# An attention with two expert layers: a weight quarter of the second layer converted earlier, GpSimd's pairs planned as longer, and the whole order planned anew

## The chip, the core and the metric

The kernel runs on one core of a Trainium2 chip. Its engines work side by side, each through its own queue in order: TensorE (PE, matmuls, with PEld its weight loads), VectorE (DVE), ScalarE (ACT), GpSimd (POOL) and SyncE (SP, whose queue here issues transfers). The metric is the device time of one execution in microseconds; before the change it is 805.47 us (median of 3 runs, 804.94 to 806.22).

## The reference

The input is a batch of 2 with 8 heads, 768 rows and 64 columns a head: 16 heads in all, counted 0 to 15 below. A row may attend to a column only if both fall into the same of 64 buckets, which six signs of a projection name. Two expert layers follow on the 1536 tokens of width 512, each with an inner width of 2048:

```python
    scores = np.where(mask, scores, -1000000000.0)
    attn = np.exp(scores - max); attn = attn / (sum + 1e-09)
    x = attn @ v                                  # 1536 x 512
    h = x @ w_in;  g = np.maximum(h, 0) + alpha * np.minimum(h, 0);  x = g @ w_out
    h = x @ w_in2; g = P(h) / (Q(h) + 1e-06);                        out = g @ w_out2
```

P is a cubic and Q a sum of absolute terms up to the square. The weights are float32.

## The kernel before

**Attention.** For each head: `load` of q and k (L428), copies rounded for TensorE (`qh`, `k2`) and their remainders (`ql`, `kx`), a small matmul for the bucket bits (`pb`, L440), whose signs VectorE writes as `bt` (L445) and two pairs of small transfers put beside `ql` and `k2` (L456). For each of six row blocks of 128: scores (`s`, L508 and L510), VectorE's scaling and minimum into `x` (`clamp`, L516), ScalarE's exponential (L522), the turn by TensorE (`t`, L540), and the copy out of PSUM into `pt` (`put`, L398 on ScalarE, L402 on VectorE). Then the product with v (`pv`, L600, 24 matmul records a head) and, on VectorE, its product with the reciprocal sums `rs` into the accumulator `acc` (`over`, L606). Heads 0 to 7 are the first batch, 8 to 15 the second.

**Expert layers.** The tokens stand in four blocks of 384 (`c` = 0 to 3), the inner width in four quarters (`Q`). One block with one quarter is a unit: four groups of twelve matmuls `h` (L626), each followed by the layer's function, its rounded result `gh` and remainder `gl` (L407), then the second product (L642 in layer one: four groups of twelve; L645 in layer two: three groups of twelve) and its sum into `acc` (L752). Every product is made of three, high x high, high x low and low x high, so each weight is split into a high and a low part. The block of tokens is split in the same way (`xh`, `xl`). Blocks 0 and 1 are complete after the first batch, so the first two units of layer one (8 groups of first and 8 of second products) can run inside the second batch; block 2 and 3 need the last head.

**Layer two's function** (`act2`) needs twelve steps for each 128 x 384 tile; two of them, the pair `a_mul` and `a_sum` (L691), have both inputs in SBUF and may run on VectorE or GpSimd.

**Conversion.** A piece is 128 x 512 weights. It is loaded (`raw`, L297), ScalarE takes two steps (L303, L307), VectorE five `bits` steps (L316, L318, L320, L322, L324) and the low part (L331); the high part is a copy. Pieces of layer one's quarters go straight into the two weight slots. Pieces of layer two's quarters 1 to 3 (kind `f`) are written out to DRAM (`spill`, two transfers, L341) and loaded back as a whole when their slot is free (`reload`, L851). They are listed in groups of eight pieces before the first unit of layer one's quarters 1, 2 and 3, and run beside its units and on into layer two.

**Order.** Nothing is ordered by hand: `Plan.order` (L159) lists every step with its engines, the time it is planned to take there, its buffers and its dependences, and lays the steps out one after the other by a rank plus a bias for each kind of step (table `FAVOUR`, from L62, with factors on the planned time by engine). Steps marked `dve` and `pool` may not overlap in the plan (`PORT`); steps marked `dvp` may. The order so found is written into each engine's queue.

Of the kernel before, what the change touches and what calls it, by code (L numbers as in the profile page):

```python
# [31 lines left out]

SCALE = 0.125
# [34 lines left out]
    "bits0": (90.6, {"pe": 3.82}), "bits_at": (-21, {"dvp": 3}), "bits_ev": (-33.5, {"dvp": 0.62}),
    "bits_evb": (-78.9, {"dvp": 0.26}), "bits_mv": (-44, {"dma": 1.35}), "bits_mvb": (-4.7, {"dma": 0.6}),
    "bitsb": (-0.2, {}), "c_abs": (-7.3, {"act": 4.44}), "c_bits": (-9.8, {"dve": 1.83}),  # L70
    "c_hi": (-117.1, {"act": 1.07, "dve": 0.06, "pool": 0.99}), "c_lo": (46.3, {}),
    "c_load": (-3, {"none": 1.84, "dma": 0.23}), "c_prep": (-65.8, {"dve": 0.95}), "c_tail": (11.2, {"act": 2.79}),
    "clamp": (23.3, {"dvp": 1.27}), "clampb": (58.9, {}), "expo": (103.2, {"act": 0.04}), "expob": (101.7, {}),
    "eye": (-39.8, {"dma": 0.68}), "eye_prep": (155.9, {"act": 0.75, "dve": 1.1, "pool": 17.07}),
    "f_abs": (-39, {"act": 4.38}), "f_bits": (-17.4, {"dve": 0.56}), "f_lo": (144.3, {"dve": 0.18}),
    "f_load": (103.9, {"dma": 1.28}), "f_out": (-90.4, {"dma": 0.94}), "f_tail": (-117.2, {"act": 1.73}),
    "flip": (-3.2, {"pe": 4.43}), "flipb": (3.4, {"pe": 1.26}), "g_both": (-103.1, {"dvp": 2.51}),
    "g_both0": (21.2, {"dvp": 1.02}), "g_both1": (0, {"dvp": 0.4}), "g_hi": (-79.1, {"act": 0.29, "dvp": 0.92}),
    "g_hi0": (-79, {"act": 13.81, "dvp": 1.84}), "g_hi1": (-119.5, {"act": 1.19, "dvp": 34.31}),
    "g_hi2": (-66.3, {"act": 0.41, "dvp": 1.12}), "g_lo": (37.8, {}), "g_lo0": (16.3, {"dvp": 0.87}),  # L80
    "g_lo1": (-19.1, {"dvp": 0.66}), "g_lo2": (1.9, {"dvp": 13.24}), "g_neg": (-11, {"act": 0.21}),
    "g_neg0": (41.3, {"act": 0.81}), "g_neg1": (-43.2, {"act": 0.52}), "guard": (-3.1, {"dve": 1.65}),
    "guardb": (-64.9, {}), "k2": (0, {"act": 1.56, "dve": 0.92, "pool": 0.43}),
    "k20": (-19, {"act": 1.86, "dve": 2.23}), "k2b": (69.6, {"act": 1.23, "dve": 5.81, "pool": 1.59}),
    "kx": (-37.8, {"dve": 1.12}), "kx0": (119.3, {}), "load": (117.4, {"dma": 0.14}),
    "load0": (-13.1, {"dma": 1.39, "none": 1.92}), "loadb": (149.1, {"dma": 5.03}),
# [162 lines left out]
def lsh_attention_moe_moe(ctx: ExitStack, tc: tile.TileContext, qT, kT, vN, consts, eye,  # L249
# [93 lines left out]
    def pieces(slot, moe, Q, parts=(0, 1)):  # L343
        return [Piece(slot, moe, Q, part, i) for part in parts for i in range(4)]
# [646 lines left out]
```

## Time and profile before

| | us |
|---|---|
| median of the runs | 805.47 (804.94 to 806.22) |
| the profiled execution | 804.19 |
| its span, first to last instruction | 802.4 |
| PE busy | 777.6 (97%) |
| DVE busy | 687.9 (86%) |
| ACT busy | 563.7 (70%) |
| POOL busy | 141.0 (18%) |
| mean granted TensorE clock | 0.997 |

Busy time is the time in which at least one instruction of the engine is under way; matmuls overlap, so the ends of a busy stretch are modelled. In the chain of work that ended last TensorE has 73%, VectorE 14%, ScalarE 7%. The first products of both layers (L626) are the largest line of the chain.

### The profile page before, as it was taken

To read this page: it belongs to the slowest core of one execution; us is meant where nothing else is said; L and a number is where in the kernel's file an instruction comes from. 1 tells how busy PE (TensorE), PEld (TensorE's weight loads), DVE (VectorE), ACT (ScalarE), POOL (GpSimd) and SP (SyncE) were. 2 spreads that over 40 slices of the span, in tenths; PEclk is the share of its full clock that TensorE was granted. 3 is DMA by queue.
4 is the path that set the end of the run, shared out by engine and by line. 5 is a ranking of instruction groups with operands and counts; after the bars stand their busy time and mean duration, and the time that the engine had idled before them with its cause. 6 is when DMAs were issued, how large, how long until landed. Compare 5 with 4: busy or idle time off the path is not lost.

```text
span 802.4 us, 12469 instructions
## 1 busy us (share of the span) xinstructions
PE 777.6 (97%) x4444; PEld 680.9 (85%) x4444; DVE 687.9 (86%) x1348; ACT 563.7 (70%) x1093; POOL 141.0 (18%) x151
## 2 busy tenths in 40 slices
PE   8999999999999889999999999999998989999998
PEld 5676676878877589999999999988997879889986
DVE  6998998675674699898899989999999999899883
ACT  3897897776675766652464436689999978887880
POOL 3343320000000000000000001056233454121120
PEclk9999999999999999999999999999999999999999
DMA  5334233121210123336543555422405361200012
GB/s 203 107 103 136 94 113 110 44 64 44 63 44 5 36 96 105 105 98 187 162 132 106 164 166 174 179 80 106 155 4 166 111 209 40 105 1 1 14 52 92
DMA packets 27134, 79.79 MB, mean 99 GB/s; under 512 B 3696, under 2 KB 4416, under 8 KB 25536
## 3 DMA queue, kind: packets, MB, share of 16 engines
q1 hardware_dynamic: 26784, 78.58, 30.5%
q8 instruction: 35, 0.57, 0.3%
q10 hardware_dynamic: 288, 0.41, 0.1%
q14 instruction: 27, 0.22, 0.1%
HBM read 62.14 MB, written 15.73 MB: 97 GB/s over the span
## 4 chain that ended last, share of the span: by engine, by line
PE 73%; DVE 14%; ACT 7%; issue 2%; POOL 2%; DMA 1%; SPq 1%; DVEq 0%; ACTq 0%; POOLq 0%
PE h L626 24%; PE o L642 14%; PE o L645 10%; PE pv L600 7%; PE t L540 6%; PE s L508 4%; PE s L510 3%; PE h L642 2%; DVE h L688 2%; DVE x L516 1%; PE pb L440 1%; DVE h L682 1%; DVE mag L322 1%; DVE gl L407 1%; DVE h L706 1%
## 5 line engine op out<-in xcount | busy, mean ns | idle before, releaser
L626 PE MATMUL h<-xh,wih 128*128 128x384 f32 x512 | 174.3, 340 | 12.1 <-DVE gl L407 8.1
L626 PE MATMUL h<-xl,wih 128*128 128x384 f32 x512 | 172.9, 338 | 0.0
L626 PE MATMUL h<-xh,wil 128*128 128x384 f32 x512 | 172.7, 337 | 0.0
L516 DVE TENSOR_SCALAR_CACHE_REDUCE x<-s 128x768 f32<-128x768 f32 x96 | 91.6, 954 | 28.2 <-PE s L510 26.2
L626 PEld LDWEIGHTS h<-xh,wih 128*128 128x128 f32 x512 | 96.7, 189 | 17.1 <-DVE gl L407 11.5
L398 ACT ACTIVATE pt<-t 128x768 f32<-128x768 f32 x92 | 73.9, 807 | 38.7 <-PE t L540 38.4
L626 PEld LDWEIGHTS h<-xh,wil 128*128 128x128 f32 x512 | 96.7, 189 | 0.7
L626 PEld LDWEIGHTS h<-xl,wih 128*128 128x128 f32 x512 | 96.6, 189 | 0.0
L522 ACT ACTIVATE x<-x,st 128x768 f32<-128x768 f32 x96 | 89.0, 928 | 6.4 <-DVE x L516 6.2
L540 PE MATMUL t<-eyes,x 128*128 128x128 f32 x576 | 79.1, 274 | 1.9 <-DVE x L516 1.1
L540 PEld LDWEIGHTS t<-eyes,x 128*128 128x128 f32 x576 | 66.4, 140 | 12.6 <-ACT x L522 4.2
L645 PE MATMUL o<-woh,gl 128*128 128x512 f32 x192 | 75.5, 393 | 0.0
L645 PE MATMUL o<-woh,gh 128*128 128x512 f32 x192 | 75.5, 393 | 0.0
L645 PE MATMUL o<-wol,gh 128*128 128x512 f32 x192 | 75.5, 393 | 0.0
L642 PE MATMUL o<-gh,woh 128*128 128x384 f32 x224 | 75.3, 336 | 0.0
L642 PE MATMUL o<-gl,woh 128*128 128x384 f32 x224 | 75.3, 336 | 0.0
L642 PE MATMUL o<-gh,wol 128*128 128x384 f32 x224 | 75.3, 336 | 0.0
L691 POOL TENSOR_TENSOR ap<-ap,t 128x384 f32<-128x384 f32 x41 | 45.6, 1113 | 168.9 <-ACT ap L679 162.3
L407 DVE TENSOR_TENSOR gl<-h,gh 128x384 fp32r<-128x384 f32 x128 | 68.8, 550 | 5.7 <-ACT gh L398 5.3
L600 PE MATMUL pv<-pt,vr 128*64 128x384 f32 x384 | 68.2, 493 | 0.0
L752 DVE TENSOR_TENSOR acc<-acc,o 128x384 f32<-128x384 f32 (+1 forms) x84 | 50.6, 603 | 14.8 <-PE o L645 10.0
L398 ACT ACTIVATE gh<-h 128x384 fp32r<-128x384 f32 x114 | 53.4, 492 | 12.9 <-DVE h L706 6.9
(111 smaller groups left out, 1628.6 us busy)
## 6 DMA issues: line engine op xcount, KB each, us to landing
raw<-w_in SPq DMA_DIRECT2D x32, 512.0 KB
raw<-w_out SPq DMA_DIRECT2D x32, 512.0 KB
rk<-kT SPq DMA_DIRECT2D x16, 384.0 KB
sp<-w SPq DMA_DIRECT2D x24, 256.0 KB
sp<-mag SPq DMA_DIRECT2D x24, 256.0 KB
rq<-qT SPq DMA_DIRECT2D x15, 384.0 KB
vr<-vN SPq DMA_DIRECT2D x8, 384.0 KB
wih<-sp SPq DMA_DIRECT2D x3, 1024.0 KB
```

Source lines behind the costliest of these rows:

```text
L398: s_.activation(out, in_, AF.Copy, scale=scale)
L407: eng[e].tensor_tensor(out, a, b, op=ALU.subtract)
L508: te.matmul(sp[:, j, :HALF], K["qh"][:, q], K["kx"][:, j * HALF:(j + 1) * HALF], start=True, stop=False)
L516: v_.tensor_scalar(x.rearrange("p (j c) -> p j c", j=2), T["s"][:, :, :HALF], SCALE, FAR, op0=ALU.mult, op1=ALU.min, accum_out=T["st"])
L522: s_.activation(T["x"], T["x"], AF.Exp, bias=T["st"], scale=-1.0, accum_out=tr["ss"][:, tt, half:half + 1])
L540: te.transpose(o[:, c], T["x"][:, c], idf)
L600: te.matmul(T["pv"][64 * half:64 * half + 64, :HALF], tv["vr"][:, m, kt, :], E[half][0]["pt"][:, kt, :], start=(kt == 0), stop=(kt == NT - 1))
L626: te.matmul(o, wt[:, kc, f], xt[:, kc], start=(n == 0), stop=(n == 3 * KC - 1))
L642: te.matmul(op[:, :HALF], lt[:, m, d], rt, start=(n == 0), stop=(n == 3 * FT - 1))
L645: te.matmul(op[:, :], lt[:, d], rt[:, m], start=(n == 0), stop=(n == 3 * FT - 1))
L691: eng[e].tensor_tensor(P[a], P[a], P[b], op=op)
L752: v_.tensor_tensor(a, a, o, op=ALU.subtract if moe else ALU.add)
```

## The change

Three things are changed. The eight pieces of layer two's quarter 1 are converted as a new kind `e`, listed right after layer one's first quarter, and no longer before layer one's quarter 1; the plan puts them into heads 9 to 15. A pair on GpSimd is planned at 1.10 us instead of 0.97. And the table `FAVOUR` holds other numbers throughout, with entries for the new kind, so that the order of all queues is another. In the changed kernel the lines stand some lines lower, four in most of the kernel: L606 is L610 there, L316 to L331 are L320 to L335, L398 and L402 are L402 and L406, L691 is L695.

```diff
+EARLY = (1,)
+
...
-    "a_log": (0, {"act": 0.25}), "a_mul": (-301.7, {"dve": 0.05, "pool": 0.26}), "a_n1": (-0, {"dvp": 1.42}),
...
+    "a_g": (21.3, {"dvp": 0.8}), "a_log": (-38.3, {"act": 0.32}), "a_mul": (-28.8, {"dve": 0.28}),
...
-        PAIR = {"pool": 0.97, "dve": 0.47}
+        PAIR = {"pool": 1.1, "dve": 0.47}
...
     convert("w", pieces(0, 0, 0, (0,)))
     convert("w", pieces(0, 0, 0, (1,)))
+    for Q in EARLY:
+        convert("e", pieces(None, 1, Q))
...
                 convert("c", pieces(0, 1, 0), (), (0,))
-            convert("f", pieces(None, 1, Q), (), (0,))
+            if Q not in EARLY:
+                convert("f", pieces(None, 1, Q), (), (0,))
```

The computation is the same, and so is the number of matmuls. Between engines some work changes hands: `ql` is all on VectorE (16 of 16, before 8), GpSimd has 65 of the 128 pair operations (before 77).

**VectorE in the attention's second batch.** Before, between the fourth row block of head 12 (`x12_3`) and the remainder `kx` for head 14:

```order
L516 TENSOR_SCALAR x12_3_2422,st12_3_2423<-s12_3_2410 128x768
L445 TENSOR_SCALAR bt13_2437<-pb13_2425,every_86 128x384
L516 TENSOR_SCALAR x12_4_2446,st12_4_2447<-s12_4_2431 128x768
L606 TENSOR_TENSOR acc2_62<-pv11_2396,rs11_2408 64x384
L606 TENSOR_TENSOR acc3_63<-pv11_2396,rs11_2408 64x384
L516 TENSOR_SCALAR x12_5_2481,st12_5_2482<-s12_5_2463 128x768
L432 SCALAR_TENSOR_TENSOR kx14_2501<-k214_2479,low_90,rk14_2449 128x768
```

Now, from the fifth row block of head 11 on (`mag`, `w32` and `raw` are the tiles of a conversion piece):

```order
L520 TENSOR_SCALAR x11_4_2251,st11_4_2252<-s11_4_2236 128x768
L320 TENSOR_SCALAR mag_2254<-mag_2254 128x512
L322 TENSOR_SCALAR mag_2254<-mag_2254 128x512
L324 SCALAR_TENSOR_TENSOR w32_2271<-raw_2082,mag_2254 128x512
L326 SCALAR_TENSOR_TENSOR mag_2254<-raw_2082 128x512
L520 TENSOR_SCALAR x11_5_2288,st11_5_2289<-s11_5_2273 128x768
L436 SCALAR_TENSOR_TENSOR kx13_2293<-k213_2291,low_90,rk13_2241 128x768
L328 TENSOR_SCALAR raw_2082<-w32_2271 128x512
L406 CAST qh13_2304<-rq13_2278 128x768
```

The steps of a piece now stand between the row blocks of a head, one piece for about each head from 9 on.

**ScalarE at the end of the attention.** Before, from the exponential of the last head's last row block on:

```order
L522 ACTIVATE x15_5_3021,ss15_0_2915<-x15_5_3021,st15_5_3022 128x768
L303 ACTIVATE mag_3039<-raw_1555 128x512
L398 ACTIVATE rr15_3052<-ss15_0_2915 128x6
L398 ACTIVATE pt15_3_3026<-t15_4_3029 128x6x128
L398 ACTIVATE pt15_3_3026<-t15_5_3042 128x6x128
L398 ACTIVATE xh2_3016<-acc2_62 128x384
L398 ACTIVATE wih1_3018<-w32_3062 128x512
L398 ACTIVATE rs15_3077<-rb15_3058 128x384
L398 ACTIVATE xh2_3016<-acc2_62 128x384
L307 ACTIVATE raw_3049<-raw_3049 128x512
L398 ACTIVATE xh2_3016<-acc2_62 128x384
```

Now, from behind the same exponential on, where `acc1<-h` is the copy of a finished second-product group of layer one's block 1:

```order
L402 ACTIVATE acc1_61<-h_3100 128x384
L307 ACTIVATE mag_3129<-raw_2889 128x512
L402 ACTIVATE pt15_3_3113<-t15_4_3120 128x6x128
L402 ACTIVATE pt15_3_3113<-t15_5_3131 128x6x128
L402 ACTIVATE wih1_3092<-w32_3162 128x512
L402 ACTIVATE acc1_61<-h_3146 128x384
L311 ACTIVATE raw_3143<-raw_3143 128x512
L307 ACTIVATE mag_3180<-raw_3143 128x512
L402 ACTIVATE wih1_3092<-w32_3197 128x512
L311 ACTIVATE raw_3185<-raw_3185 128x512
L402 ACTIVATE acc1_61<-h_3201 128x384
```

Three of the four copies of block 1's groups stand in these rows, around the last head's last `pt` copies and behind them; the fourth is four rows earlier. Before, none is left here.

**VectorE at the last head's product.** Before, up to the product of the last head with its sums (`acc2<-pv15`, `acc3<-pv15`):

```order
L324 TENSOR_SCALAR raw_1555<-w32_3062 128x512
L331 SCALAR_TENSOR_TENSOR wil1_3019<-mag_3039,raw_1555 128x512
L407 TENSOR_TENSOR xl2_3017<-acc2_62,xh2_3016 128x384 x2
L316 TENSOR_SCALAR mag_3086<-mag_3086 128x512
L318 TENSOR_SCALAR mag_3086<-mag_3086 128x512
L320 SCALAR_TENSOR_TENSOR w32_3093<-raw_3049,mag_3086 128x512
L322 SCALAR_TENSOR_TENSOR mag_3086<-raw_3049 128x512
L324 TENSOR_SCALAR raw_3049<-w32_3093 128x512
L331 SCALAR_TENSOR_TENSOR wil1_3019<-mag_3086,raw_3049 128x512
L606 TENSOR_TENSOR acc2_62<-pv15_3070,rs15_3077 64x384
L606 TENSOR_TENSOR acc3_63<-pv15_3070,rs15_3077 64x384
```

Now, from the sums' copy (`rs15`) on:

```order
L406 COPY rs15_3194<-rb15_3166 128x384
L322 TENSOR_SCALAR mag_3180<-mag_3180 128x512
L324 SCALAR_TENSOR_TENSOR w32_3197<-raw_3143,mag_3180 128x512
L326 SCALAR_TENSOR_TENSOR mag_3180<-raw_3143 128x512
L610 TENSOR_TENSOR acc2_62<-pv15_3168,rs15_3194 64x384
L328 TENSOR_SCALAR raw_3143<-w32_3197 128x512
L406 CAST xh2_3090<-acc2_62 128x384
L610 TENSOR_TENSOR acc3_63<-pv15_3168,rs15_3194 64x384
L411 TENSOR_TENSOR xl2_3091<-acc2_62,xh2_3090 128x384
L335 SCALAR_TENSOR_TENSOR wil1_3093<-mag_3180,raw_3143 128x512
```

Six steps of a piece stood right ahead of `acc2<-pv15`; now three do, behind the copy of the sums, and the splits of block 2 (`xh2`, `xl2`) follow at once.

**GpSimd in layer two.** Before:

```order
L691 TENSOR_TENSOR ap_6182<-ap_6182,t_6179 128x384
L691 TENSOR_TENSOR ap_6258<-ap_6258,t_6255 128x384
L691 TENSOR_TENSOR al_6252<-al_6252,ap_6258 128x384
L691 TENSOR_TENSOR ap_6339<-ap_6339,t_6336 128x384
L691 TENSOR_TENSOR al_6333<-al_6333,ap_6339 128x384
L691 TENSOR_TENSOR ap_6423<-ap_6423,t_6417 128x384
L691 TENSOR_TENSOR al_6414<-al_6414,ap_6423 128x384
L691 TENSOR_TENSOR ap_6506<-ap_6506,t_6503 128x384
L691 TENSOR_TENSOR al_6496<-al_6496,ap_6506 128x384
```

Now, in the second quarter of the layer:

```order
L695 TENSOR_TENSOR al_6482<-al_6482,ap_6475 128x384
L695 TENSOR_TENSOR ap_6532<-ap_6532,t_6543 128x384
L695 TENSOR_TENSOR al_6540<-al_6540,ap_6532 128x384
L695 TENSOR_TENSOR al_6616<-al_6616,ap_6613 128x384
L695 TENSOR_TENSOR ap_6642<-ap_6642,t_6674 128x384
L695 TENSOR_TENSOR al_6645<-al_6645,ap_6642 128x384
L695 TENSOR_TENSOR al_6671<-al_6671,ap_6667 128x384
L695 TENSOR_TENSOR al_6696<-al_6696,ap_6693 128x384
L695 TENSOR_TENSOR al_6814<-al_6814,ap_6808 128x384
```

In the rows before, GpSimd has both operations (`ap`, the product, and `al`, the sum) of nearly every tile; in the rows now, the sum of seven tiles and the product of two.

## Rows read from the trace of the kernel before

**Rows 1.** Stages of the span: PE, PEld, DVE, ACT, POOL busy (instructions), clock, DMA share, GB/s.

```profile
0.00:25.00 25.00, 21.17 (x106) 16.41 (x106) 18.45 (x36) 12.55 (x23) 7.87 (x16) 1.00 0.55 185
25.00:125.00 100.00, 98.39 (x675) 69.99 (x675) 92.52 (x189) 85.30 (x161) 34.79 (x39) 1.00 0.37 112
125.00:268.00 143.00, 141.33 (x912) 109.55 (x910) 91.09 (x185) 95.41 (x175) 3.18 (x5) 1.00 0.16 48
268.00:290.00 22.00, 16.09 (x90) 12.53 (x87) 18.85 (x41) 16.14 (x32) 0.00 (x0) 0.92 0.24 73
290.00:515.00 225.00, 225.00 (x1290) 225.00 (x1289) 206.95 (x411) 117.42 (x228) 4.95 (x6) 1.00 0.46 143
515.00:665.00 150.00, 141.90 (x724) 128.40 (x723) 146.80 (x274) 137.84 (x279) 65.61 (x62) 1.00 0.34 115
665.00:780.00 115.00, 115.00 (x578) 103.88 (x577) 103.93 (x202) 96.75 (x196) 22.67 (x23) 1.00 0.09 35
780.00:802.40 22.40, 18.66 (x83) 15.12 (x81) 9.27 (x16) 2.25 (x5) 1.93 (x2) 0.97 0.25 94
```

**Rows 2.** Waits, 268 to 290 us: total us, times, longest.

```profile
PE h L626 <- DVE acc L606: 4.0, 1, 4.0
```

**Rows 3.** Order of time, 268 to 290 us: start, us, engine, instruction, [idle before <-releaser].

```profile
276.65 4.16 PE L600 MATMUL pv<-pt,vr 128*64 128x384 f32 x24
...
280.00 0.43 DVE L316 TENSOR_SCALAR mag<-mag 128x512 f32<-128x512 f32 x1
...
283.55 1.14 DVE L606 TENSOR_TENSOR acc<-pv,rs 64x384 f32<-64x384 f32 x2
...
284.84 0.42 PE L626 MATMUL h<-xh,wih 128*128 128x384 f32 x1 [4.03 <-DVE acc L606]
```

**Rows 4.** Waits, 515 to 665 us.

```profile
PE h L626 <- DVE gl L407: 8.1, 8, 2.8
```

**Rows 5.** Groups, VectorE, 515 to 665 us: busy us, mean ns | idle before.

```profile
L322 DVE SCALAR_TENSOR_TENSOR mag<-raw 128x512 uint32<-128x512 uint32 x11 | 10.2, 932 | 0.0
L320 DVE SCALAR_TENSOR_TENSOR w<-raw,mag 128x512 uint32<-128x512 uint32 x10 | 8.8, 878 | 0.0
...
L316 DVE TENSOR_SCALAR mag<-mag 128x512 f32<-128x512 f32 x10 | 6.5, 661 | 0.0
...
L331 DVE SCALAR_TENSOR_TENSOR mag<-mag,raw 128x512 fp32r<-128x512 uint32 x7 | 6.4, 911 | 0.0
```

**Rows 6.** Groups, VectorE, 290 to 475 us, the same lines.

```profile
L320 DVE SCALAR_TENSOR_TENSOR w<-raw,mag 128x512 uint32<-128x512 uint32 x34 | 23.4, 687 | 0.4
L322 DVE SCALAR_TENSOR_TENSOR mag<-raw 128x512 uint32<-128x512 uint32 x33 | 22.7, 687 | 0.5
...
L316 DVE TENSOR_SCALAR mag<-mag 128x512 f32<-128x512 f32 x34 | 14.3, 421 | 2.6 <-ACT mag L303 2.4
...
L331 DVE SCALAR_TENSOR_TENSOR mag<-mag,raw 128x512 fp32r<-128x512 uint32 x13 | 8.9, 687 | 0.1
```

**Rows 7.** Groups of the whole span, shapes kept apart.

```profile
L691 POOL TENSOR_TENSOR ap<-ap,t 128x384 f32<-128x384 f32 x41 | 45.6, 1113 | 168.9 <-ACT ap L679 162.3 <-DVE h L706 3.0 <-DVE h L688 2.3
...
L303 ACT ACTIVATE mag<-raw 128x512 f32<-128x512 f32 x64 | 42.9, 671 | 23.8 <-DMA raw<-w_out 9.1 <-DMA raw<-w_in 8.5 <-DVE mag L322 2.8
...
L691 DVE TENSOR_TENSOR ap<-ap,t 128x384 f32<-128x384 f32 x23 | 12.8, 555 | 1.7 <-ACT ap L679 1.6
...
L407 DVE TENSOR_TENSOR ql<-qh,rq 64x768 fp32r<-64x768 f32 x8 | 7.6, 944 | 0.0
...
L402 DVE COPY rs<-rb 128x384 f32<-128x384 f32 x8 | 4.4, 553 | 0.0
...
L402 DVE COPY pt<-t 128x768 f32<-128x768 f32 x4 | 3.8, 953 | 0.0
```

**Rows 8.** Waits of SP's queue, 125 to 268 us.

```profile
SPq L428 <- PE pb L440: 72.0, 6, 13.5
SPq L456 <- DVE bt L445: 18.6, 6, 16.8
```

**Rows 9.** The chain that ended last: a group of twelve matmuls in the attention.

```profile
175.70 2.11 PE h L642 x12
```

More of the change, by code (lines that the diff above doesn't have):

```diff
@@ L68 @@
[L68 to L86, printed above, removed]
-    "o_add1": (-96.6, {"dvp": 0.26}), "o_add2": (-45.5, {"dvp": 1.41}), "o_ev": (-42.9, {"act": 0.69, "dvp": 0.06}),
-    "o_ev0": (201.1, {"act": 1.59}), "o_ev2": (-1.3, {"act": 0.01, "dvp": 0.71}), "over": (-6.9, {"dvp": 0.75}),
@@ L95 @@
-    "recip": (-4.5, {"dve": 18.1}), "recipb": (0, {"dve": 1.29}), "reload": (67.7, {}), "s1": (146.1, {"pe": 0.36}),
-    "s10": (-6.1, {}), "s11": (105.8, {"pe": 1.24}), "s12": (171.3, {}), "s2": (195.1, {}),
-    "s20": (1.4, {"pe": 1.76}), "s21": (90, {"pe": 0.23}), "s22": (60.5, {"pe": 0.47}),
-    "scaled": (-5.6, {"act": 634.44, "dvp": 1.3}), "scaledb": (7.5, {"act": 1.72, "dvp": 1115.1}),
-    "scores": (0, {"pe": 1.2}), "scoresb": (0, {"pe": 0.64}), "spread": (31.9, {"pe": 3.11}),
-    "store": (-140, {"dma": 2.58}), "swap": (-103.8, {"none": 0.81}), "take": (192.2, {"act": 0.74}),
@@ new lines @@
+    "a_prep": (-62.3, {"dve": 6.68}), "a_quad": (168, {"dvp": 0.92}), "a_sq": (-50.8, {"act": 0.64}),
+    "a_sum": (-162.9, {"dve": 1.41, "pool": 1.05}), "back": (0, {"act": 1.47, "dvp": 2.21}),
+    "backb": (37.6, {"act": 4.4, "dvp": 1.76}), "banks": (36.2, {"none": 3.86}), "bits": (94, {"pe": 0.11}),
+    "bits0": (-39.1, {"pe": 0.72}), "bits_at": (28.3, {"dvp": 0.48}), "bits_ev": (0, {"dvp": 0.44}),
+    "bits_evb": (-12.3, {}), "bits_mv": (89.5, {"dma": 0.68}), "bits_mvb": (61.9, {}), "bitsb": (-32.1, {}),
@@ new lines @@
+    "load0": (16.7, {"dma": 0.62, "none": 0.49}), "loadb": (-8.4, {"dma": 0.39}), "o_add1": (-82.2, {"dvp": 1.3}),
+    "o_add2": (1.5, {"dvp": 0.43}), "o_ev": (-61.1, {"dvp": 3.22}), "o_ev0": (123.5, {"act": 0.74, "dvp": 0.91}),
+    "o_ev2": (80.6, {"act": 0.61, "dvp": 0.41}), "over": (-29.3, {"dvp": 0.41}), "overb": (-89.7, {"dvp": 0.15}),
+    "part1": (0, {"act": 0.15}), "part1b": (-35, {"act": 1.86, "pool": 2.51}), "part2": (-76, {"dve": 0.14}),
+    "part2b": (45.2, {"dve": 0.31, "pool": 1.2}), "pv": (-149.3, {"pe": 0.82}), "pvb": (-33.3, {"pe": 15.25}),
@@ new lines @@
+    "scaled": (202.1, {"act": 0.01}), "scaledb": (-469.6, {"act": 8.42, "dvp": 1.36}), "scores": (-100.3, {}),
+    "scoresb": (-7, {}), "spread": (-82.1, {"pe": 0.67}), "store": (0, {"dma": 1.45}),
+    "swap": (-133.1, {"none": 1.59}), "take": (0, {"act": 0.04, "dvp": 1.28}),
+    "takeb": (141.7, {"act": 2.85, "dvp": 170.19}), "turn": (213.3, {"pe": 1.51}), "turnb": (83.8, {"pe": 0.65}),
+    "u_abs": (13.3, {}), "u_bits": (-86.7, {"dve": 2.17}), "u_hi": (3, {"act": 0.01, "dve": 0.47, "pool": 1.39}),
@@ L109 @@
+    "x_lo2": (-148.8, {"dve": 2.22, "pool": 2.04}),
 }
```

49 lines of the change are left out of this document (31 added, 18 removed).

## The prediction

> **What bounds the kernel now.** I read the stages first, then the waits in the two stages where TensorE idles, then the instructions inside them. Over the span TensorE is busy 777.6 of 802.4 us, so only about 25 us can be won at all; the table of stages [rows 1] says where they lie. Subtract PE busy from the length of each stage: 3.8 us at the start, 1.6 in 25 to 125 (the attention's first batch), 1.7 in 125 to 268 (its second batch), 5.9 in 268 to 290 (the last head, then the first layer's second half), nothing in 290 to 515, 8.1 in 515 to 665 (end of layer one and the first half of layer two), nothing in 665 to 780, 3.7 at the end. Two holes matter. A busy TensorE is no proof of full use, but the first batch gives a yardstick: it runs with VectorE busy 92.5 of 100 us and still idles TensorE only 1.6%.
>
> In the first hole TensorE waits 4.0 us for L606 in one piece [rows 2]. L606 multiplies the last head's product into `acc`; the next matmuls need it. The order of time [rows 3] shows why it is late: the last `pv` runs from 276.65 to 280.81, VectorE then begins a whole conversion piece at 280.00 and reaches L606 only at 283.55, and the matmul starts at 284.84. No other matmul was left to run: all eight second-product groups of layer one's first two units were used up before. The hole also costs clock: the granted clock is 0.92 over these 22 us, where the stages around it have 1.00 [rows 1], so 0.08 x 22 = 1.8 us on top. The hole is worth 5.9 + 1.8 = 7.7 us.
>
> In the second hole TensorE waits eight times, 8.1 us, for `gl` (L407) [rows 4], the VectorE step that frees a PSUM buffer. VectorE is busy 146.8 of 150 us there [rows 1]: it is the bound. Part of that is no work. L322, L320, L316 and L331 take 932, 878, 661 and 911 ns in this stage [rows 5] and 687, 687, 421 and 687 in layer one, where GpSimd is nearly idle [rows 6]. With their counts that is 11 x 0.245 + 10 x 0.191 + 10 x 0.240 + 7 x 0.224 = 8.6 us of stretch, beside 65.6 us of GpSimd work.
>
> The Trainium skill (SBUF — State Buffer, section "SBUF: two separate sides") says that VectorE and GpSimd share one port pair under an exclusive lock, and that a loser waits until the winner's instruction is over. The trace agrees: conversion instructions, which read and write SBUF alone, stretch up to 1.57 fold (661 against 421 ns).
>
> **The change, part by part.** All sums are against the profiled execution, 804.19 us (span 802.4), which lies 1.28 us under the median of 805.47.
>
> *Eight conversion pieces move from layer one into heads 9 to 15.* Each is six VectorE instructions, two ScalarE ones, one load and two spills. A piece takes VectorE 3.55 us back to back (280.00 to 283.55) [rows 3], so 8 x 3.55 = 28.4 us at most. The moved work left a stage in which TensorE never waited (290 to 515), so leaving it gains nothing there by itself. Where it goes, VectorE is busy 91.1 of 143 us [rows 1]; TensorE has four groups of twelve matmuls fewer there, 4 x 2.1 = 8.4 us [rows 9] that now stand with the last head, so it becomes about 119.5 of 134.6 us, 89%: under the 92.5% of the yardstick. ScalarE gets 16 x 0.671 = 10.7 us [rows 7] on 95.4, about 79%. SP gets 24 more transfers, queued among `rk`, `rq` and the small `k2`/`ql` moves that the next head's scores need; but SP waited 72.0 + 18.6 us in this stretch for PE's and VectorE's products [rows 8], so it has room, and a spill holds the rows behind it only as long as its own conversion is late. Price: nothing, if PE stays the bound, to 2.5 us (the yardstick's 1.6% of 143, rounded up); I take 0.5, as the share stays below the yardstick's.
>
> *First batch, order anew.* Eight `ql` subtractions go from GpSimd to VectorE: 8 x 0.944 = 7.6 us. Ten casts (`k2`, `xh`) come, at most 10 x 0.553 = 5.5; seven `rs` copies leave, 7 x 0.553 = 3.9, and four `pt` copies, 4 x 0.953 = 3.8 [rows 7]. Net at most +5.4 us on 92.5, less two conversion instructions and a cast, some 1.6: 96 of 100. Less GpSimd work also means less stretch. Price 0 to 3.6 us; I take 1.0, nearer to the low end since PE idled 1.6 us at 92.5.
>
> *The end of the attention.* In the new order four second-product groups of twelve matmuls stand with the last head, three of them between its steps and one behind the last `pv`; before there was one with the last head and none behind. VectorE now has `rs15`, three conversion instructions, then L606, `xh`, L606, `xl`. Since `rs15` and the three lie beside the last six `pv` matmuls (2.1 us), L606 starts right after `pv`; L606, one conversion step, a cast and then the second L606 and `xl`, five instructions no longer than the 0.55 us of a copy of this size [rows 7], take 2.8 us at most, of which the group covers 2.1. So 0.7 us is left here, and about a microsecond before it (the chain through softmax of the last head). Without a long pause I expect the clock to stay at its full level (1.00, the 2.4 GHz level). Gain 7.7 - 1.7 = 6.0; bounds 3.0 (if the loads come late and the groups are spent before) and 7.7.
>
> *Layer two.* Counted in the two orders from the first matmul of layer two to the point where 114 us of matmuls are left: conversion instructions 63 before, 54 now; pair operations (L691) on GpSimd 63, now 41; on VectorE 16, now 34; casts of `gh` on VectorE 5, now 1. VectorE: -9 x 0.6 - 4 x 0.55 + 18 x 0.555 = +2.4 us. Stretch: none where GpSimd does nearly nothing [rows 6], 8.6 us with 63 pairs and 63 conversion instructions [rows 5]; scaled with both counts 8.6 x (41/63) x (54/63) = 4.8, saving 3.8. Net -1.4 us. Besides, the planner prices a pair on GpSimd at 1.10 instead of 0.97, and the trace has 1.113 [rows 7]: before, each pair ended 0.14 us later than the order was made for, now 0.01. That can take away some of the 4.8 left; I take 1.1, about a quarter. Gain 2.5; bounds -2.4 (stretch unchanged, VectorE 2.4 longer) and 8.1 (no wait left).
>
> The Trainium skill (Perfetto Trace Analysis, section "Optimizing Scalar/DVE Operations") speaks against this part: it says that work may be offloaded from a saturated VectorE to GpSimd, and that between these two it might not help. Here the change does the reverse on the saturated engine. By its first half the sum for layer two would be the +2.4 us of VectorE work, by its second half about zero; the rows put it at -1.4.
>
> Start and tail keep their order but for a few instructions: 0, with 0.5 either way.
>
> Sum: -6.0 - 2.5 + 1.0 + 0.5 = -7.0 us; profiled 797.2, median **798.5 us**.
>
> **The rivals.**
> 1. *Layer two gives nothing.* VectorE's 18 pairs eat what the conversions and the lock give back, and `gl` stays the bound. For it: the net of -1.4 us is small beside 146.8. Against it: the price of a pair on GpSimd is now right. 805.47 - 6.0 + 1.5 = 801.0.
> 2. *Both holes close.* Layer two then follows the plan and TensorE loses 1 us there instead of 8.1. For it: conversions end 19 us of matmul work earlier than before, and stage 665 to 780, with VectorE at 90%, has no idle at all. 805.47 - 6.0 - 7.1 + 1.5 = 793.9.
> 3. *VectorE becomes the bound of the attention: slower.* The place is its queue in heads 1 to 14, where conversion steps and `ql` stand ahead of L516, for which the transposes' exponentials wait. What a VectorE-bound stretch costs is to be read in 515 to 665: 5.4% idle. If both batches went so, 3.8% of 100 and 4.2% of 143 us are lost more, 9.8 us. With layer two unimproved: 805.47 - 6.0 + 9.8 = 809.3. It decides when the loss passes 6 us, some 0.43 us for each of 14 heads. For it: 96% in the first batch, close to the 97.9% of the bound stage. Against it: the second batch stays at 89%, and GpSimd's share falls from 34.8 us.
> 4. *It doesn't do what it says at the end of the attention:* the load for the third `w_in` piece comes late, ScalarE stands before it, VectorE's conversion steps wait, and L606 behind them. Then the groups run dry and half the hole stays: 805.47 - 3.0 - 2.5 + 1.5 = 801.5.
>
> **How the numbers follow.** Forecast (796 to 800) 0.40, rival 1 0.16, rival 2 0.20, rival 3 0.10, rival 4 0.09, the rest, with several small losses, 0.05 (about 805). A measurement of this kernel can tell about 0.2%, 1.6 us, from no change. Faster: 0.40 + 0.16 + 0.20 + 0.09 = 0.85, less 0.02 for their upper ends: 0.83. Same 0.07. Slower 0.10. The range from 791.5 to 804 takes in the low end of rival 2, and rivals 1 and 4; it leaves out rival 3, the rest and the far ends of layer two's bounds.
>
> **What would show it.** The first hole: TensorE idle in the 22 us around the last `pv` under 2 us and no granted clock below 1.00 there; a wait for L606 of over 1 us says rival 4. Layer two: L322, L320, L316 and L331 nearer to their layer-one times, and the wait for `gl` between 3 and 7 us; 8 or more says rival 1, under 2 rival 2. Attention: first and second batch together idle TensorE no more than 5 us; VectorE over 97% there, with waits of PE for L516 that add up to several us, says rival 3. The forecast is wrong as a whole if the last `pv` ends later by what the holes give back.

## The result, and the profile after

The changed kernel takes 792.17 us (median of 4 runs, 791.45 to 794.5). Against the kernel before on the same chip (805.21) the ratio is 0.9846, 95% interval 0.9817 to 0.9876: faster by 13.0 us. The profiled execution took 791.45 us, its span is 789.5 and its granted clock 1.000 throughout.

The stages of the changed kernel, cut at the same times as [rows 1] (columns as there; the last stage ends with the span):

```profile
0.00:25.00 25.00, 21.10 (x106) 16.38 (x106) 18.67 (x37) 14.78 (x27) 4.33 (x13) 1.00 0.56 188
25.00:125.00 100.00, 98.43 (x675) 69.84 (x677) 91.06 (x199) 87.68 (x163) 16.65 (x25) 1.00 0.37 111
125.00:268.00 143.00, 139.32 (x895) 104.04 (x892) 112.83 (x233) 101.99 (x189) 8.29 (x14) 1.00 0.36 107
268.00:290.00 22.00, 21.99 (x133) 18.66 (x131) 20.41 (x48) 13.51 (x25) 1.01 (x1) 1.00 0.25 73
290.00:515.00 225.00, 225.00 (x1291) 225.00 (x1290) 203.06 (x402) 115.63 (x224) 6.54 (x9) 1.00 0.35 110
515.00:665.00 150.00, 148.60 (x761) 135.52 (x760) 145.80 (x284) 135.26 (x276) 46.70 (x46) 1.00 0.32 113
665.00:780.00 115.00, 115.00 (x569) 102.78 (x568) 95.87 (x183) 88.03 (x180) 25.41 (x25) 1.00 0.11 40
780.00:789.50 9.50, 5.81 (x26) 4.49 (x24) 2.06 (x3) 0.00 (x0) 0.00 (x0) 1.00 0.22 83
```

Take PE busy from the length of each stage again. The end of the attention idles 0.0 us (5.9 before), 515 to 665 idles 1.4 (8.1 before), the attention's second batch idles 3.7 (1.7 before); start, first batch and tail are as they were. Idle time fell from 24.9 to 14.3 us, 10.6 us. PE busy fell from 777.55 to 775.24, 2.3 us, about what the two stages with a lower clock had cost (0.08 x 22 + 0.03 x 22.4 = 2.4 us); no stage has a clock below 1.00 any more. Together they make the 12.9 us by which the span is shorter. VectorE's second batch went from 91.1 to 112.8 us: there the early conversion went.

The end of the attention in order of time (compare [rows 3]): the last half of the value product, the group of second products behind it (its first matmul), L606 (now L610), and the first matmul of the next block.

```profile
276.95 2.16 PE L604 MATMUL pv<-pt,vr 128*64 128x384 f32 x12
279.04 0.44 PE L646 MATMUL h<-gh,woh 128*128 128x384 f32 x1
279.51 0.55 DVE L610 TENSOR_TENSOR acc<-pv,rs 64x384 f32<-64x384 f32 x1
...
281.44 0.44 PE L630 MATMUL h<-xh,wih 128*128 128x384 f32 x1
```

No bracket, no idle time: the group runs while VectorE takes its products. The next block begins 2.4 us behind the value product (279.04 to 281.44). The wait for `gl`, which was 8.1 us [rows 4], in the waits of TensorE over the whole span:

```profile
PE h L630 <- DVE gl L411: 1.4, 4, 0.6
```

The conversion steps in 515 to 665 us (compare [rows 5]; L320 is the old L316, L324 the old L320, L326 the old L322, L335 the old L331):

```profile
L326 DVE SCALAR_TENSOR_TENSOR mag<-raw 128x512 uint32<-128x512 uint32 x10 | 7.9, 791 | 0.0
L335 DVE SCALAR_TENSOR_TENSOR mag<-mag,raw 128x512 fp32r<-128x512 uint32 x8 | 6.5, 817 | 0.0
L324 DVE SCALAR_TENSOR_TENSOR w<-raw,mag 128x512 uint32<-128x512 uint32 x8 | 6.0, 759 | 0.0
...
L320 DVE TENSOR_SCALAR mag<-mag 128x512 f32<-128x512 f32 x8 | 3.9, 500 | 0.0
```

Against the means of [rows 6] the stretch is 10 x 0.104 + 8 x 0.130 + 8 x 0.072 + 8 x 0.079 = 3.3 us, before 8.6. So far it looks as if fewer pairs on GpSimd had freed VectorE. The experiments say otherwise.

### The profile page after: what moved, and what is told of

Its sections match the earlier page's. It is cut to its first block, busy times and chain, and to the rows that moved or that the text cites. A ratio compares the mean times of both kernels' runs of the same rounds, so it can differ in the third digit from the quotient of the medians.

```text
span 789.5 us, 12492 instructions
## 1 busy us (share of the span) xinstructions
PE 775.2 (98%) x4444; PEld 676.7 (86%) x4444; DVE 689.8 (87%) x1384; ACT 556.9 (71%) x1076; POOL 108.9 (14%) x132
## 4 chain that ended last, share of the span: by engine, by line
PE 72%; DVE 11%; ACT 8%; DMA 5%; issue 2%; SPq 1%; POOL 0%; DVEq 0%; ACTq 0%; POOLq 0%
PE h L630 25%; PE o L646 13%; PE o L649 11%; PE pv L604 6%; PE t L544 6%; PE s L512 4%; PE s L514 3%; PE h L646 2%; DMA rq<-qT 2%; DVE h L692 2%; DMA raw<-w_in 2%; DVE x L520 1%; PE pb L444 1%; SPq L460 1%; ACT aq L689 1%
## 5 line engine op out<-in xcount | busy, mean ns | idle before, releaser
L402 ACT ACTIVATE pt<-t 128x768 f32<-128x768 f32 x96 | 77.1, 807 | 30.6 <-PE t L544 29.8
L402 ACT ACTIVATE gh<-h 128x384 fp32r<-128x384 f32 x111 | 52.6, 491 | 24.6 <-DVE h L710 11.7
L666 ACT ACTIVATE t<-h 128x384 f32<-128x384 f32 x64 | 31.1, 486 | 44.4 <-PE h L630 44.3
```

The source lines that it names most:

```text
L402: s_.activation(out, in_, AF.Copy, scale=scale)
L666: s_.activation(P["r"], P["h"], AF.Relu, scale=-1.0)
```

## The experiments

Two questions stood open. What closed layer two's hole: fewer GpSimd pairs beside the conversions (theory C), the early conversion (D), or the new price of a pair? And what closed the hole at the end of the attention: the order of VectorE, or the product groups? In the first experiments one thing is moved by hand in the list that the planner returns, so that all else keeps its place.

### Fewer pairs on GpSimd, in the kernel before

```diff
     order = plan.order()
+    last = max(n for n, t in enumerate(order) if t.kind == "f_lo")
+    some = [t for t in order[:last] if t.kind == "a_mul" and t.eng == "pool"]
+    for n, t in enumerate(some):
+        if n % 3 < 2:
+            t.eng = "dve"
```

> The kernel before, its order kept, but that 22 of the 60 two-input operations of the second expert layer that GpSimd carries beside conversions (two of three products L691, by position) run on VectorE: nearly the change's own count of GpSimd pairs there (36 in the changed kernel, 38 here), with the conversions left where they are. Theory C, the pairs on GpSimd stretch VectorE's conversion steps: these fall towards their times of layer one (878 to about 760 ns, 932 to about 790 ns), the wait for gl falls from 8.1 us to 1 to 4 us, and the time to 798 to 801 us, although VectorE is given 22 x 0.56 = 12 us of work. Theory D, the gain of the changed kernel there comes from the conversions that were done early: VectorE, 98% busy in that stretch, gets 12 us more, the wait for gl grows, 808 to 817 us.

Measured: 808.29 us, ratio 1.0033 (1.0016 to 1.005): 0.3% slower. Groups of 515 to 665 us, the stage's row, and TensorE's wait:

```profile
L320 DVE SCALAR_TENSOR_TENSOR w<-raw,mag 128x512 uint32<-128x512 uint32 x11 | 9.2, 839 | 0.0
L322 DVE SCALAR_TENSOR_TENSOR mag<-raw 128x512 uint32<-128x512 uint32 x11 | 7.4, 680 | 0.0
...
L316 DVE TENSOR_SCALAR mag<-mag 128x512 f32<-128x512 f32 x11 | 5.2, 479 | 0.0
```

```profile
515.00:665.00 150.00, 142.88 (x729) 129.03 (x728) 148.37 (x293) 135.81 (x273) 40.73 (x42) 1.00 0.35 118
```

```profile
PE h L626 <- DVE gl L407: 8.9, 10, 1.8
```

The stretch shrinks in two of these steps as theory C has it (932 to 680 ns, 661 to 479) and hardly in the third (878 to 839). But the operations themselves weigh more than what they gave back: VectorE is 1.6 us busier, the wait for `gl` stays, and the time is theory D's.

### More pairs on GpSimd, in the changed kernel

```diff
     order = plan.order()
+    last = max(n for n, t in enumerate(order) if t.kind == "f_lo")
+    for t in order[:last]:
+        if t.kind == "a_mul" and t.eng == "dve":
+            t.eng = "pool"
```

> The changed kernel, its order kept, but that the 23 products of a pair that VectorE carries there beside conversions run on GpSimd (59 pairs there instead of 36, as in the kernel before); the early conversion stays. Theory C, GpSimd's pairs stretch the conversion steps: the steps' means rise again to 850 to 930 ns, the wait for gl from 1.4 to 4 to 8 us, the time to 796 to 800 us. Theory D, the early conversion made the gain: VectorE is relieved by 23 x 0.56 = 13 us, the wait for gl stays under 1.5 us and the time is 790 to 793 us.

Measured: 791.13 us, ratio to the kernel before 0.9825 (0.98 to 0.985): as the changed kernel. The stage's row and the wait:

```profile
515.00:665.00 150.00, 148.99 (x764) 136.10 (x763) 139.77 (x265) 136.33 (x277) 67.80 (x66) 1.00 0.33 113
```

```profile
PE h L630 <- DVE gl L411: 1.0, 4, 0.4
```

GpSimd is as busy as before the change (67.8 against 65.6 us), and the hole stays closed. Two of the four conversion steps grow (L326 from 791 to 872 ns, L324 from 759 to 797), less far than theory C has it, and VectorE is still 6.0 us less busy than in the changed kernel. Theory C falls from both sides. The Trainium skill (Perfetto Trace Analysis, section "Optimizing Scalar/DVE Operations") says that offloading from a saturated VectorE to GpSimd may make sense and that between these two it might not help. In the kernel before, the run agrees with its first half: taking 22 operations back from GpSimd cost 0.33%. In the changed kernel, where TensorE hardly waits for VectorE, giving GpSimd 23 more changed nothing.

### Each half of the change alone, with a table of its own

The table was found for one set of steps and costs. So a random search over its numbers, which keeps what shortens the plan's own span, was run for each half alone until it stopped gaining. The diffs are against the changed kernel.

```diff
-        PAIR = {"pool": 1.1, "dve": 0.47}
+        PAIR = {"pool": 0.97, "dve": 0.47}
...
 FAVOUR = {
...
```

> The early conversion alone: GpSimd's pairs stay planned at 0.97 us as in the kernel before, and the table that sets the order is searched anew for this combination until it no longer gains. 56 pairs stand on GpSimd beside conversions (before 60, changed kernel 36); the end of the attention comes out as in the changed kernel, one product group behind the last value product. Theory E, the early conversion is the whole gain, in both holes: no idle time at the end of the attention, the wait for gl under 2.5 us, 789 to 793 us. Theory P, the layer-two part comes from planning GpSimd's pairs as longer: the wait for gl stays at 5 us or more and the time is 796 to 800 us.

Measured: 791.66 us, ratio 0.9831 (0.9813 to 0.9849). No wait over 0.6 us at the end of the attention, 1.3 us for `gl`: the early conversion with a table of its own brings the whole gain, in both holes.

```profile
PE h L632 <- DVE gl L413: 1.3, 2, 0.7
```

And the price alone:

```diff
-EARLY = (1,)
+EARLY = ()
...
 FAVOUR = {
...
```

> The longer GpSimd pairs alone: the second quarter is converted in layer one as in the kernel before, pairs are planned at 1.1 us, and the table is searched anew for this combination. The end of the attention comes out as before (nothing behind the last value product), and 78 pairs stand on GpSimd beside conversions. Theory E: both holes stay, 5 us or more at the end of the attention and 6 us or more of waits for gl, 803 to 809 us. Theory P: the hole of layer two closes without the early conversion, the wait for gl is under 3 us and the time 797 to 801 us.

Measured: 802.01 us, ratio 0.996 (0.9944 to 0.9975). TensorE's waits, and one group of 515 to 665 us:

```profile
PE h L632 <- DVE acc L612: 3.5, 1, 3.5
PE h L632 <- DVE gl L413: 3.3, 3, 2.1
```

```profile
L328 DVE SCALAR_TENSOR_TENSOR mag<-raw 128x512 uint32<-128x512 uint32 x11 | 7.7, 708 | 0.0
```

The first hole stays; the wait for `gl` falls to 3.3 us, neither theory's number, and neither is the time: the whole wins 0.4%. So a new order with the new price closes more than half of layer two's hole without the early conversion. On top of the early conversion the price is worth nothing that can be measured (791.66 against 792.17).

Each half has one searched table. Two orders with the early conversion take 791.66 and 792.17 us, two without it 802.01 and 805.21. How much a single search scatters was not measured, and the table searched anew with neither half was not run.

### The end of the attention, one engine at a time

First VectorE's order alone, in the kernel before:

```diff
+    over = [t for t in order if t.kind == "overb"][-2:]
+    order = [t for t in order if t not in over]
+    at = max(n for n, t in enumerate(order) if t.kind == "pvb")
+    while order[at - 1].kind == "u_bits":
+        at -= 1
...
+    order[at:at] = [last, *over]
```

> The kernel before, its order kept, but for VectorE at the end of the attention: the two products of head 15's output with its scales (L606) and the last half of its value product stand ahead of the six steps of the conversion piece that they followed. Theory A, the wait of 4.0 us on L606 is an order of VectorE: the products run at about 281 us, as the last value product ends, the next expert block begins some 2.5 us sooner, its wait falls to about 1.5 us, and the time to about 802.7 us. Theory B, TensorE lacks other work there and whatever VectorE does first, something else is late (the splits of the accumulators, the scales): the idle time stays within 1 us of 5.9 us and the time within 1 us of 805.2 us.

Measured: 805.41 us, ratio 1.0 (0.9985 to 1.0015). TensorE's two waits, then ScalarE, in order of time:

```profile
281.17 0.41 PE L626 MATMUL h<-xh,wih 128*128 128x384 f32 x1 [1.31 <-DVE acc L606]
285.74 0.69 PE L626 MATMUL h<-xh,wih 128*128 128x384 f32 x1 [2.77 <-ACT xh L398]
```

```profile
282.70 0.63 ACT L398 ACTIVATE wih<-w 128x512 fp32r<-128x512 f32 x1 [3.69 <-DVE w L320]
...
285.18 2.16 ACT L398 ACTIVATE xh<-acc 128x384 fp32r<-128x384 f32 x5
```

The wait for L606 falls to 1.3 us as theory A says, and a wait of 2.8 us for `xh` takes its place: ScalarE's splits stand behind its own steps of the conversion piece, the first of which waits 3.7 us for a VectorE step that is now later. Together 4.1 us, as before, and the time is theory B's. The wait is a chain over three queues.

Then the product groups alone, in the kernel before: the last four, one behind each of head 15's last three transposes and one behind its last value product.

```diff
+    ours = [t for t in order if t.kind in ("s20", "o_ev0")][-8:]
+    order = [t for t in order if t not in ours]
+    flips = [n for n, t in enumerate(order) if t.kind == "flipb"]
+    last = max(n for n, t in enumerate(order) if t.kind == "pvb")
+    for n, group in ((last, ours[6:]), (flips[-1], ours[4:6]), (flips[-2], ours[2:4]), (flips[-3], ours[:2])):
+        order[n + 1:n + 1] = group
```

> The kernel before, its order kept, but that the last four product groups of the second expert unit (48 matmuls and the four copies behind them) stand one behind each of the last three transposes of head 15 and one behind its last value product, as in the changed kernel, instead of in heads 12 to 14. Filler theory: TensorE has work in both idle pieces of the end of the attention, idle time there falls from 5.9 us to under 1.5 us, the granted clock stays at 1.00, and that is worth up to 7.7 us; heads 12 to 14 lose the groups as cover and idle 1 to 4 us more; the time is 798 to 802 us. Rival, the groups hide as much where they stood: the idle time only moves, 804 to 807 us. Second rival, VectorE's order holds the next block in any case: the wait on L606 stays above 2 us behind the last group.

Measured: 814.14 us, ratio 1.0099 (1.0073 to 1.0125): slower than any case foresaw.

```profile
125.00:268.00 143.00, 138.04 (x891) 105.13 (x890) 88.40 (x180) 97.42 (x179) 3.13 (x5) 1.00 0.15 46
268.00:290.00 22.00, 14.72 (x86) 12.24 (x85) 15.20 (x33) 9.55 (x20) 0.00 (x0) 0.96 0.19 55
```

```profile
PE s L508 <- DVE x L516: 5.1, 9, 0.8
PE h L626 <- DVE acc L606: 3.7, 1, 3.7
```

The groups are missed where they stood (six of the nine waits for `x` lie in 200 to 268 us; the second batch idles 5.0 us). Behind the last group the wait for L606 is 3.7 us after all, as the second rival has it. VectorE still takes the conversion piece first, and it also stands for the groups themselves: in the kernel before, their copies (`acc<-h`) are in VectorE's queue, in the changed kernel seven of the eight are ScalarE's. Two of the four, in VectorE's order of time:

```profile
269.31 0.56 DVE L402 COPY acc<-h 128x384 f32<-128x384 f32 x1 [3.84 <-PE h L642]
...
285.84 0.56 DVE L402 COPY acc<-h 128x384 f32<-128x384 f32 x1 [1.55 <-PE h L642]
```

The second stands ahead of three steps of the piece and of L606. So this run doesn't tell what the groups alone would do with their copies on ScalarE.

Third, the chain on all three engines, with one group behind the last value product:

```diff
+    s2, ev = [t for t in order if t.kind in ("s20", "o_ev0")][-2:]
+    hi = next(t for t in order[order.index(last):] if t.kind == "x_hi")
+    lo = next(t for t in order if t.kind == "x_lo" and hi in t.deps)
+    ev.eng = "act"
+    ours = [last, s2, *over, hi, lo, ev]
...
+    order = front + ours + [t for t in order[at:] if t not in ours]
```

> The kernel before, its order kept, but for the chain at the end of the attention on three engines at once: one product group of the second unit stands behind the last value product on TensorE, the two products L606 and the split of the accumulator that the next block needs stand ahead of the conversion piece on VectorE and on ScalarE (where that split waited behind the piece's steps). Theory A2, the wait is a chain over in-order queues and closes only when all of it is moved: idle time behind the last value product falls from 4.0 us to under 1 us, the clock stays at 1.00, and the time falls by 2.5 to 5 us to 800 to 802.5 us. Theory B2, a hole closed by hand there only moves (the group is missed where it stood, the delayed conversion piece holds the blocks behind it): 804 us or more.

Measured: 805.74 us, ratio 1.0004 (0.999 to 1.0019). The only idle time of TensorE between 277 and 300 us:

```profile
292.21 0.69 PE L626 MATMUL h<-xh,wih 128*128 128x384 f32 x1 [3.01 <-DVE gl L407]
```

The hole is closed, and opens again some eight microseconds later, for `gl`, whose VectorE steps stand behind the conversion piece that was put off. The first `gl` behind the hole, in the kernel before and in this run:

```profile
292.54 0.55 DVE L407 TENSOR_TENSOR gl<-h,gh 128x384 fp32r<-128x384 f32 x1
```

```profile
291.61 0.55 DVE L407 TENSOR_TENSOR gl<-h,gh 128x384 fp32r<-128x384 f32 x1
```

TensorE begins the block 4.3 us sooner (280.56 against 284.84 us), but VectorE reaches `gl` only 0.9 us sooner. Another 1.2 us are lost where the group was taken away: the second batch idles 2.9 us, before 1.7. Theory B2 holds. In the kernel before, VectorE owed this work, and the hole was only the place where TensorE paid.

Last the reverse, in the changed kernel: its group behind the last value product put ahead.

```diff
+    ours = [t for t in order if t.kind in ("s20", "o_ev0")][-2:]
+    order = [t for t in order if t not in ours]
+    at = max(n for n, t in enumerate(order) if t.kind == "o_ev0") + 1
+    order[at:at] = ours
```

> The changed kernel, its order kept, but that the product group behind the last value product stands ahead of head 15's last stretch, behind the group that precedes it. If that group is what hides the chain from the value product over VectorE and ScalarE to the next block, TensorE idles 1.3 to 2.2 us behind the last value product and the time is 793 to 795 us; if VectorE's order alone does it, the idle time stays under 0.5 us and the time within 1 us of 791.5 us.

Measured: 796.51 us, ratio 0.9895 (0.9874 to 0.9915), 4.3 us above the changed kernel.

```profile
285.09 0.45 PE L630 MATMUL h<-xh,wih 128*128 128x384 f32 x1 [3.95 <-DVE acc L610]
```

```profile
268.00:290.00 22.00, 18.05 (x102) 15.01 (x101) 16.03 (x38) 9.68 (x17) 1.01 (x1) 0.92 0.23 73
```

The old wait of 4.0 us is back, with its clock of 0.92, and here it costs 4.3 us. That is more than either case foresaw, because the edit moves more than cover. The group's copy on ScalarE now waits for the group ahead of two steps of the next piece:

```profile
278.81 0.49 ACT L402 ACTIVATE acc<-h 128x384 f32<-128x384 f32 x1 [3.97 <-PE h L646]
```

VectorE stands 4.7 us for those steps, and L606 begins 2.0 us behind the value product instead of 0.4. About 2.4 us of the wait is the missing cover, the stretch that the group fills in the changed kernel; the rest comes with the edit. So the group is needed, and in these runs it pays only where VectorE is not behind.

### VectorE's load, put back and taken away

In the changed kernel, one conversion step is done twice on each of the 40 pieces between the attention and layer two:

```diff
+                for again in range(2 if (self.moe, self.to[0]) not in ((0, 0), (1, 1), (1, 3)) else 1):
-                v_.scalar_tensor_tensor(w, self.top, 0xC0000000, m, op0=ALU.bitwise_and, op1=ALU.bitwise_or)
+                    v_.scalar_tensor_tensor(w, self.top, 0xC0000000, m, op0=ALU.bitwise_and, op1=ALU.bitwise_or)
```

> The changed kernel, its order kept, with one VectorE step (the sign-and-magnitude step L324, repeated on the same operands) added to each of the 40 weight pieces that are converted between the attention and layer two: 40 x 0.69 = 28 us of VectorE work, about what the early conversion took out of layer one (8 pieces x 6 steps). Theory V, the gain is room on VectorE between the attention and the last conversion: the room is gone, waits for gl come back at the start of layer one and in layer two, 5 to 14 us in all, 797 to 806 us. Rival, the gain is where the instructions stand (the product groups beside head 15, the earlier start of layer two), which this leaves alone: TensorE's idle time grows by less than 2 us and the time is 790 to 794 us.

And on every other piece:

```diff
-                for again in range(2 if (self.moe, self.to[0]) not in ((0, 0), (1, 1), (1, 3)) else 1):
+                for again in range(2 if self.to[2] % 2 == 0 and (self.moe, self.to[0]) not in ((0, 0), (1, 1), (1, 3)) else 1):
```

> As the run before, on every other of these pieces: 20 x 0.69 = 14 us of VectorE work. Theory V with a margin: 292 to 798 us over 790, that is 792 to 798 us, and less than half of the loss of the full dose, since VectorE idles 22 us in layer one of the changed kernel. Rival: 790 to 793 us.

(The first number there, 292, is a slip for 792.) Measured: 807.2 us, ratio 1.0028 (1.0013 to 1.0044), with 40 steps; 796.91 us, ratio 0.9905 (0.9881 to 0.9929), with 20. The stage of layer one with 40 steps, and TensorE's wait, first with 40, then with 20:

```profile
290.00:515.00 225.00, 217.42 (x1233) 214.58 (x1232) 213.37 (x413) 104.15 (x207) 2.62 (x4) 1.00 0.34 106
```

```profile
PE h L631 <- DVE gl L412: 11.0, 12, 2.9
```

```profile
PE h L631 <- DVE gl L412: 4.1, 7, 2.0
```

Theory V holds; with 40 steps the time lies 1.2 us above its range. The first 14 us cost 4.7, the next 14 us 10.3: VectorE had a margin there, and not a large one. With 28 us the whole gain is gone. Most of the new waits lie in layer one (7.6 us of 225), which idled nowhere before.

The reverse, in the kernel before: five of the six VectorE steps of the second quarter left out, nothing moved. The second weight quarter of layer two is then not the reference's.

```diff
         def bits(self, j):
+            if self.slot is None and self.to[0] == 1 and j != 2:
+                return
...
         def low_part(self):
+            if self.slot is None and self.to[0] == 1:
+                return
```

> The kernel before, its order kept, with five of the six VectorE steps of each of the eight pieces of the second quarter left out where they stand, in layer one (its second weight quarter is thus not the reference's): 40 steps, some 24 us less for VectorE, and nothing moved. If the amount of VectorE's work in layer one decides, the waits for gl in layer two fall from 8 to under 4 us and the time to 798 to 802 us. If the gain needs the order that the room allows (later pieces pulled forward, layer two begun sooner), TensorE, which is 100% busy there in any case, gets nothing: the waits stay within 1.5 us of 8 us and the time is 803 to 807 us.

Measured: 805.36 us, ratio 1.0007 (0.999 to 1.0024).

```profile
290.00:515.00 225.00, 225.00 (x1291) 225.00 (x1290) 188.86 (x371) 116.67 (x228) 4.94 (x6) 1.00 0.46 143
```

```profile
PE h L630 <- DVE gl L411: 8.0, 9, 2.8
PE h L630 <- DVE acc L610: 4.0, 1, 4.0
```

VectorE is 18 us less busy in layer one, and not one wait is shorter. With every queue's order kept, the room is worth nothing.

### Two quarters early

```diff
-EARLY = (1,)
+EARLY = (1, 2)
...
 FAVOUR = {
...
```

> The changed kernel with the third quarter converted early too (16 pieces instead of 8 during the attention), the table searched anew for it. Theory V: VectorE is 112.8 us of 143 busy in the attention's second batch, another 8 pieces add some 26 us, 97%: the attention's end is late by 5 us or more, and the time is 794 to 803 us, although the holes of layer two stay closed. Rival, there is room for more and each quarter taken out of layer one is worth some us: 784 to 790 us.

Measured: 808.07 us, ratio 1.0034 (1.0017 to 1.0051), above the range.

```profile
25.00:125.00 100.00, 91.83 (x615) 64.26 (x614) 93.79 (x193) 85.69 (x157) 20.02 (x28) 1.00 0.44 133
125.00:268.00 143.00, 141.62 (x924) 109.35 (x923) 114.30 (x238) 108.61 (x198) 19.60 (x20) 1.00 0.41 128
```

It loses, but not where I put the loss: VectorE is at 114 of 143 us in the second batch, and TensorE idles 8.2 us in the first one, into which the new order moved the first early pieces (the first spill is issued at 90 us). That is 6.6 of the 12.4 us by which TensorE idles more than in the changed kernel; more is lost at the start and in 268 to 515 us, and the second batch gains 2.3 us. Whether two quarters are too many for the attention, or only this order is poor, stays open.

## Why the prediction was right, and where not

The direction, the places and the range (791.5 to 804) held; the number, 798.5, was 6.3 us high. By the prediction's own sign, a wait for `gl` under 2 us, it was rival 2 that came (both holes close, 793.9, chance 0.20). The range held, by 0.7 us, because it took in the low end of that rival; the mechanism that the forecast gave for layer two did not carry it.

**The end of the attention: right, for the reason given.** Taken 6.0, measured 7.7 (idle 5.9 to 0.0, clock 0.92 to 1.00), the upper bound. L606 begins 0.4 us behind the last matmul of the value product and the group covers the rest; the microsecond set aside for head 15's softmax chain wasn't needed. Putting the group back brings the hole back. What the prediction didn't see is that nearly the same hole, closed in the kernel before, only moves: I priced it as if it were TensorE's own.

**Eight pieces into heads 9 to 15: priced within the bound, the worth of leaving misjudged.** Taken 0.5, bound 2.5; measured 2.0 us more idle time in the second batch, with VectorE at 112.8 of 143 us, 79%. The 89% of the prediction took four groups out of that stage; the trace has three fewer there (96 records of second products before, 60 now), which alone makes it 87%. But the sentence "The moved work left a stage in which TensorE never waited (290 to 515), so leaving it gains nothing there by itself" was read as if it gained nothing elsewhere. By itself it does gain nothing: taking the work away without moving anything changed no wait. With a new order, the early conversion brings the whole gain.

**The first batch: too dear.** Taken 1.0, measured 0.0 (1.6 us idle before and after). VectorE came out at 91.1 of 100 us, not 96: the fall of the stretch was named but put at nothing (L316 has 750 ns there before, its like 422 now), and a cast of `xh` takes 0.36 us, not 0.55.

**Layer two: the term that was mis-sized.** Taken 2.5, measured 6.7 (8.1 to 1.4). Two steps of it failed.
- I scaled the stretch with the counts of pairs and of conversion steps. The 4.8 us that this gave came out at 3.3, but the counts are not what sets it: in the run with the new price alone L328, the old L322, takes 708 ns beside 74.8 us of GpSimd work, in the kernel before 932 beside 65.6. Which instructions meet matters as well (last section).
- I summed what VectorE gains and loses, -1.4 us, and took TensorE's gain to be of that size. VectorE's busy time did move by 1.0 us only (146.8 to 145.8). What changed besides is what TensorE had to do meanwhile. Second products in 515 to 665 us, before and after:

```profile
L645 PE MATMUL o<-woh,gl 128*128 128x512 f32 x80 | 31.6, 395 | 0.0
...
L642 PE MATMUL o<-gl,woh 128*128 128x384 f32 x16 | 5.4, 334 | 0.0
```

```profile
L649 PE MATMUL o<-woh,gl 128*128 128x512 f32 x88 | 34.7, 394 | 0.0
...
L646 PE MATMUL o<-gl,woh 128*128 128x384 f32 x24 | 8.0, 335 | 0.0
```

Twelve of layer two's take 2.77 us in the chain of the changed kernel that ended last:

```profile
638.03 2.77 PE o L649 x12
```

Each group above is a third of its products, so 24 more stand there of each kind; at 2.77 us for twelve of layer two's and 2.11 for twelve of layer one's [rows 9] they are 5.5 + 4.2 = 9.7 us of matmuls, while the first products, on which the functions hang, fell a little. A part of this is the window, as the changed kernel is ahead by its gain at the end: in 528 to 678 us of the kernel before, equally far from the end, layer two's have x88 too, and layer one's x4. So layer one's second products reach further into layer two than before, and layer two begins sooner. Its first function step (ScalarE, in order of time), before and after:

```profile
517.15 0.56 ACT L697 ACTIVATE h<-h,every 128x384 f32<-128x384 f32 x1
```

```profile
496.95 0.56 ACT L701 ACTIVATE h<-h,every 128x384 f32<-128x384 f32 x1
```

It comes at 497.72 with the early conversion alone and at 521.37 with the price alone. The eight pieces stood ahead of layer one's later weights in one line of conversions, and their leaving may have pulled that line and the start of layer two forward by 20 us. That this start and the mixture of products fill the hole is read from these rows and was not tried apart. It is not the only way: with the price alone layer two begins 4.2 us later than before, and the wait for `gl` still falls from 8.1 to 3.3 us. What exactly closes layer two's hole stays open; shown is that the early conversion with its order does, and that VectorE's load put back opens waits again.

**The price of a pair** was given 1.1 us of the loss that I left standing. Beside the early conversion it is worth nothing that could be measured.

**Rival 1** (VectorE's pairs eat the rest) and **rival 4** (late loads) didn't come: 1.4 us for `gl`, no wait at the last head. **Rival 3** didn't come either: VectorE 91% and 79% in the two batches.

**The runs point to no version that beats the changed kernel:** with more pairs on GpSimd (791.13) and with the early conversion alone (791.66) the time is the same within the intervals.

## What to carry to other kernels

An idle hole need not be where the time is lost: before you fill one, ask whether the engine waited for is behind with its work, because then closing it by hand moves it (here by some eight microseconds) and gains nothing. When you move instructions by hand, move what waits for them too, and look at whose queue that stands in. Work moved to an early stage where its engine has room can pay two stages later; here it did with an order planned anew, while taken out in place, with the order kept, it was worth nothing. And when one engine's steps are stretched beside another's, don't scale the stretch with counts: look at which instructions meet.

## What the hardware showed that I had not expected

The stretch of VectorE's conversion steps beside GpSimd's pairs followed neither count nor busy time: L322 took 932 ns in the kernel before (54 pairs in that stage, 65.6 us of GpSimd), 680 with two thirds of the products `a_mul` there moved to VectorE, and its like 708 in a run with 68 pairs (74.8 us). The single instructions show why a mean misleads. L322 in 515 to 665 us of the kernel before (shortest, median, longest in ns):

```profile
L322 DVE SCALAR_TENSOR_TENSOR mag<-raw x11: 675/683/1509, 515.1 to 659.4; 128x512 uint32<-128x512 uint32 x11
```

Seven of the eleven take 675 to 683 ns, no more than in layer one (687); four take 979 to 1509, each of them beside a running GpSimd instruction. Five of the seven short ones also run beside one for a part of their time, so meeting is not enough. The Trainium skill (SBUF — State Buffer, section "SBUF: two separate sides") speaks of an exclusive lock on a shared port. These times agree that an instruction is held up or not; a slowdown shared out evenly would not leave five of the nine that met GpSimd at their old length.
